# Head sums over eight offsets at once, and a first addend in another tile's memory, in a transformer block with dilated window attention and a gated MLP

## The chip, the core and the metric

The kernel runs on one core of a Trainium2 chip. A core has a matrix engine (PE, with its weight loads shown as PEld), a vector engine (DVE), a scalar engine (ACT), a general engine (POOL) and a synchronising engine (SP). They run side by side, each in the order of its own instruction list, and wait for each other by semaphores. Transfers (DMA) are issued from the lists of SP, POOL and ACT and carried by 16 shared DMA engines. The metric is the time of one execution in microseconds (us) on the device; lower is better.

## The reference

All tensors are bfloat16. There are S = 2048 positions of D = 1024 features, 32 heads of 32 features, a window of 8 offsets with a stride of 2, and a gated MLP with two halves of 1792 features.

```python
def _A_ref(x, wqkv, wo):                     # H, Dh, W, dil = 32, 32, 8, 2
    q, k, v = split_heads(x @ wqkv)
    idx = pos[:, None] - (jnp.arange(W) * dil)[None, :]
    logits = einsum('bhsd,bhswd->bhsw', q, k[idx]) * Dh ** -0.5
    attn = softmax(where(idx >= 0, logits, -1e9), axis=-1)
    return merge_heads(einsum('bhsw,bhswd->bhsd', attn, v[idx])) @ wo

def _B_ref(x, w_in, w_sp, b_sp, w_out):      # Fh = 1792
    z = gelu(x @ w_in)
    z1, z2 = z[..., :Fh], layernorm(z[..., Fh:])
    g = einsum('ts,bsf->btf', w_sp, z2) + b_sp[None, :, None]
    return (z1 * g) @ w_out

h = x + _A_ref(layernorm(x), A_wqkv, A_wo)
out = h + _B_ref(layernorm(h), B_w_in, B_w_sp, B_b_sp, B_w_out)
```

## The kernel before

**Tiling.** The positions are cut into four chunks of 512 (`NCH`, `CH`), a chunk into four row tiles of 128 (`TPC`). The projection to queries, keys and values gives feature-major tiles: a partition holds eight neighbouring features (`DLO`), so four partitions make a head. For an offset w, DVE multiplies the queries by the keys shifted by 2w (L414, `prod`) and adds the eight products of each partition together in three steps (L418, L421, L424, the last into `part`). PE then adds the four partitions of each head with a matrix of ones, `E32` (L442): that is the **head sum**, and its result is the logits `L` in PSUM. It is made of matmuls with 32 columns of weights, four of which stand side by side in the array.

**One chunk's attention.** Products and head sums (two groups of four offsets, `nw = 4`), then DVE's maximum (L451), subtraction (L461), ACT's exponential (L463), sums and reciprocal (L467 to L476), the weights `attn` (L485). PE spreads the weights of a head over its four partitions (L497, into `pb` and `pba`), ACT and DVE copy them to `AB` (L502). DVE multiplies the shifted values by them (L517) and adds (L525). Two of the eight additions are made by an accumulating transfer from POOL's queue (`gather`, L531): `av_z` is added to `av_y`, `av_zz` to `av_oT`. The tile `av_z` lies in the memory of the queries, `qT`; so the queries of the next chunk, which are loaded by POOL's queue (L387), must wait until that transfer is done (`G["qfree", c]`).

**Head.** PE multiplies the result by `wo` (`head`, L587); DVE adds the residual (L596) into `hb`, ACT sums the squares (L601), POOL makes the root (L560). Chunks 0 to 2 are normalised by ACT (L629) and go by one transpose transfer on SP's queue into `hnT` (L634). Chunk 3 is normalised row tile by row tile on DVE (L613), each with a transpose of its own (L619). The tiles `hnT` have one tag and two buffers of 8 KB a partition.

**Gated MLP.** `b_z2` (L660, four row tiles, each as a group of 1024 and one of 768 columns) makes the half that is normalised, ACT evicts it with the gelu (L667), squares it (L676) and normalises it (L689; DVE L691 for chunk 3), and it is stored. `b_z1` (L710) makes the other half, feature-major, ACT evicts it (L716), SP stores it (L717). When the head of chunk 3 is done, the attention's memory is given up, and the 12 row tiles of the normalised half of chunks 0 to 2 are loaded into it from POOL's queue (`z2sb`, L772). Then follow the mixing over positions (L810) and the output projection (L825), which have an order of their own and are the same in both kernels.

**What sets the order.** Everything between the first norm and L810 is put into a list of operations (`add`) with an engine, a length in us, dependencies and a priority. `Order.run` goes through them as a list scheduler, gives each a start by these lengths, and emits the instructions in the order of the starts. Waiting is not scheduled: an engine that is late on the chip keeps its order. So the lengths of the list set how the matmuls of head sums, heads and MLP stand among each other on PE. PE's accumulators (`acc`) are three, `L` is one, `part` two, `prod` two.

Of the kernel before, what the change touches and what calls it, by code (L numbers as in the profile page):

```python
# [11 lines left out]
BF16 = mybir.dt.bfloat16  # L12
# [8 lines left out]
P = 128  # L21
# [3 lines left out]
TPC = CH // P  # L25
KT = D // P
# [8 lines left out]
LMODE = (1, 1, 1, 1)  # L35
LSLACK, BSLACK = 2.0, 2.0
Z2ACT = (4, 4, 4, 0)
ACCUM_US = 12.0
PIECES = ((0, 0), (0, 4), (1, 0), (1, 4))
LNPRIO = (0, 2.0, 2.5, 4.0)  # L40
LAST_COLS = ((0, 512), (512, 768), (768, 1024))
# [85 lines left out]
def kernel(  # L127
# [13 lines left out]
    V, A, T = nc.vector, nc.scalar, nc.tensor  # L141
# [18 lines left out]
    E32 = csb[:, 128:160]  # L160
# [122 lines left out]
    add = o_.add  # L283
    G = {}
# [44 lines left out]
    def order():  # L329
        seq[0] += 1  # L330
        return 6.0 + seq[0] * 1e-3

    def qkv(c):
        for xi in range(3):
            wv = wsb[xi][:].rearrange("p kt (m dl) -> p kt dl m", dl=DLO)
            for dp in range(DLO // 2):
                key = ("acc", "qkv", c, xi, dp)
                deps = [G.get(("xnT", c))]
                if c == 0 and xi == 0 and dp < 2:
                    def mm(wv=wv, dp=dp):  # L340
                        if dp == 0:
                            accs = [new_acc(), new_acc()]
                            G["acc", "qkv", 0, 0, 0], G["acc", "qkv", 0, 0, 1] = accs
                            for kt in range(KT):
                                for dl in range(4):
                                    T.matmul(accs[dl // 2][:, dl % 2, :], wv[:, kt, dl, :], xnT[0][:, kt, :],  # L346
                                             start=(kt == 0), stop=(kt == KT - 1))
                    last = add("PE", 6.91 if dp == 0 else 0.0, mm, deps, prio=order(), take="acc")
                else:
                    for j, k0 in PIECES:  # L350
                        def mm(j=j, k0=k0, dl=2 * dp + j, wv=wv, key=key):
                            if j == 0 and k0 == 0:
                                G[key] = new_acc()
                            for kt in range(k0, k0 + 4):
                                T.matmul(G[key][:, j, :], wv[:, kt, dl, :], xnT[c][:, kt, :],  # L355
                                         start=(kt == 0), stop=(kt == KT - 1))
                        last = add("PE", 0.863, mm, deps, prio=order(), take="acc" if j == 0 and k0 == 0 else None)
                        deps = [(last, 0.0)]
                def ev(xi=xi, dp=dp, key=key):
                    if c == 0:  # L360
                        off = 0 if xi == 0 else HALO
                        A.copy(att_in[0][xi][:, 2 * dp:2 * dp + 2, off:off + CH], G[key][:])  # L362
                        if xi > 0 and dp == 3:
                            dma(qkv_d[xi][:, :, CH - HALO:CH], att_in[0][xi][:, :, CH:CH + HALO])
                    else:
                        stg = l1.tile([P, 2, CH], BF16, name="stg", tag="xn", bufs=4)
                        A.copy(stg[:], G[key][:])  # L367
                        dma(qkv_d[xi][:, 2 * dp:2 * dp + 2, c * CH:(c + 1) * CH], stg[:])
                G["ev", c, xi, dp] = add("ACT", 0.92, ev, [last], prio=2.0, free="acc", lat=0.15, take="xn" if c else None)
                if c:  # L370
                    dma_op(3.5, lambda: None, [G["ev", c, xi, dp]], free="xn")
            G["wdone", c, xi] = last
        G["qkvlast", c] = last
# [4 lines left out]
    def attention(c):  # L378
# [17 lines left out]
                G["xnT", 3].deps.append((d_v, 0.1))  # L396
        st, parts, qs, pvs = {}, {}, [{} for _ in range(W_WIN)], {}
        mode = LMODE[c]
        nw = 8 // max(mode, 2)
        lms = []  # L400
        first = G["avdone", c - 1] if c else None
        prev = None
        for g in range(W_WIN // nw):
            adds = []
            for wi in range(nw):
                w = g * nw + wi
                o = HALO - DIL * w
                def qk(w=w, wi=wi, o=o, g=g):
                    st = qs[w]
                    qT, kT = att_in[c][0], att_in[c][1]  # L410
                    if wi == 0:
                        parts[g] = att.tile([P, nw, mode, CH], BF16, name="part", tag="part", bufs=2)
                    st["prod"] = att.tile([P, DLO, CH], BF16, name="prod", tag="prod", bufs=2)
                    V.tensor_tensor(st["prod"][:], qT[:], kT[:, :, o:o + CH], op=ALU.mult)  # L414
                def add1(g=g, wi=wi, w=w):
                    p_ = qs[w]["prod"]
                    dst = parts[g][:, wi] if mode == 4 else p_[:, 0:4, :]
                    V.tensor_tensor(dst, p_[:, 0:4, :], p_[:, 4:8, :], op=ALU.add)  # L418
                def add2(g=g, wi=wi, w=w):
                    p_ = qs[w]["prod"]  # L420
                    V.tensor_tensor(parts[g][:, wi] if mode == 2 else p_[:, 0:2, :], p_[:, 0:2, :], p_[:, 2:4, :], op=ALU.add)  # L421
                def add3(g=g, wi=wi, w=w):
                    p_ = qs[w]["prod"]
                    V.tensor_tensor(parts[g][:, wi], p_[:, 0:1, :], p_[:, 1:2, :], op=ALU.add)  # L424
                pr_ = prev = add("DVE", 2.21, qk, [d_q, d_k, (prev, 0.0) if prev else None, first], prio=3.0, take=("prod", "part") if wi == 0 else "prod")
                pr_ = add("DVE", 1.13, add1, [pr_], prio=3.0, free="prod" if mode == 4 else None)
                if mode <= 2:
                    pr_ = add("DVE", 0.60, add2, [pr_], prio=3.0, free="prod" if mode == 2 else None)
                if mode == 1:
                    pr_ = add("DVE", 0.34, add3, [pr_], prio=3.0, free="prod")  # L430
                first = None
                adds.append(pr_)
            if g == W_WIN // nw - 1:
                G["qkdone", c] = adds[-1]
            slack = add("DMA", LSLACK if g < W_WIN // nw - 1 else 0.0, lambda: None, adds)
            def lm(g=g):
                if g == 0:
                    st["L"] = ps_att.tile([P, W_WIN, P], FP32, name="L", tag="L")
                L = st["L"]
                for z in range(mode):  # L440
                    for sq in range(4):
                        T.matmul(L[32 * sq:32 * sq + 32, nw * g:nw * g + nw, :], E32,  # L442
                                 parts[g][:, :, z, sq * P:(sq + 1) * P],
                                 start=(z == 0), stop=(z == mode - 1), tile_position=(0, 32 * sq))
            lms.append(add("PE", {1: 0.38, 2: 0.65, 4: 0.65}[mode], lm, [slack], prio=1.0, take="L" if g == 0 else None, free="part", lat=0.2))
        if c == 0:
            lms.append(add("DVE", 0.3, lambda: V.tensor_tensor(st["L"][0:32, :, 0:16], st["L"][0:32, :, 0:16], maskb, op=ALU.add),
                           lms, prio=3.0))
# [31 lines left out]
        for hw in range(2):  # L480
# [7 lines left out]
            for sh in range(2):  # L488
                def pbm(sh=sh, ws=ws, hw=hw):
# [5 lines left out]
                    for j in range(2):  # L495
                        sq = 2 * sh + j
                        T.matmul(pb[:, j], B4[32 * sq:32 * sq + 32, :], st["attn"][32 * sq:32 * sq + 32, ws, :],  # L497
                                 start=True, stop=True, tile_position=(32 * sq, 0))
                pm = add("PE", 0.2, pbm, [wait], prio=1.0, take="acc" if sh else "L", lat=0.2)
                eng = "DVE" if (hw == 0 and sh == 1) else "ACT"  # L500
                def cp(sh=sh, ws=ws, hw=hw, eng=eng):
                    (V.tensor_copy if eng == "DVE" else A.copy)(  # L502
# [2 lines left out]
                                   free="acc" if sh else "L", lat=0.15)  # L505
        last = prev
        av = {}
        homes = {"y": (att, "part", 2), "z": (att, "qT", 1), "zz": (bp, "hb", 1), "b": (att, "prod", 2), "p": (att, "prod", 2), "oT": (att, "oT", 1)}

        def mul(w, key):  # L510
            def f():
# [15 lines left out]
                    oTs[c] = av["oT"]  # L527
            return add("DVE", 2.30, f, deps, prio=3.0, free=free, lat=lat)

        def gather(to, key, deps):  # L530
            i_ = add("POOL", 1.1, lambda: nc.gpsimd.dma_start(av[to][:], av[key][:], accum_op=ALU.add, max_dma_last_dim=4096), deps, prio=1.0, lat=0.3)  # L531
            return add("DMA", ACCUM_US, lambda: None, [i_])

        y = dm(0, "y", [], take="part")
        z = dm(1, "z", [y])
        g1 = G["qfree", c] = gather("y", "z", [z])
        o_2 = dm(2, "oT", [z] + ([G["headmm", c - 1]] if c else []))
        z = dm(3, "zz", [o_2] + ([G["hnT", c - 1]] if c else []))
        g2 = gather("oT", "zz", [z])
        prev = dm(4, "b", [z], take="prod")  # L540
        for w in (5, 6, 7):
            m_ = dm(w, "p", [prev], take="prod" if w == 5 else None, free="part" if w == 7 else None)
# [22 lines left out]
    def head(c):  # L565
# [40 lines left out]
        if last:  # L606
            G["close"] = dma_op(0.0, close_, [G["headmm", c]] + [G["z2n", k, il] for k in range(c) for il in range(TPC)])
            for il in range(TPC):
# [6 lines left out]
                n_ = add("DVE", 0.5, nrm, [rs], prio=0.6)  # L615
                def tr(il=il):
                    if il == 0:
                        hnTs[c] = bp.tile([P, TPC, KT, P], BF16, name="hnT", tag="hnT")
                    nc.sync.dma_start_transpose(hnTs[c][:, il], st["hnc"][:, il, :].rearrange("s (a p) -> s a p", p=P))  # L619
                G["hnT", c, il] = dma_op(4.0, tr, [n_])  # L620
            G["hnT", c] = G["hnT", c, TPC - 1]
# [8 lines left out]
            nd.append(add("ACT", 1.16, nrm, [rs], prio=4.0))  # L630
        G["hdone", c] = nd[-1]
        def tr():
            hnTs[c] = bp.tile([P, TPC, KT, P], BF16, name="hnT", tag="hnT")
            nc.sync.dma_start_transpose(hnTs[c][:].rearrange("p il a s -> p (il a) s"),  # L634
                                        st["hnc"][:].rearrange("s il (a p) -> s (il a) p", p=P))
        G["hnT", c] = dma_op(8.0, tr, nd)
# [234 lines left out]
```

## Time and profile before

| | us |
|---|---|
| median of three runs | 732.07 |
| lowest and highest | 731.43, 734.21 |
| the profiled execution | 734.07 |
| its span | 732.2 |
| PE busy in the span | 723.2 |
| DVE busy | 419.3 |
| ACT busy | 220.8 |

The span counts from the first instruction of the program to its last; the execution's time has what lies around it too. "Busy" of PE counts overlapping matmuls once. The clock granted to PE was 0.995 of full over the span. A line of the form "L442 ... x32" is a group of 32 instructions of source line 442; "wait" is put down to the engine or transfer that ended it last. The page's lines of costliest groups give for the mixing (L810) 194.0 us of PE, for the two MLP halves (L660, L710) 98.5 and 98.4 us, and for the projections (L355) 56.6, 56.3 and 49.7 us. The head sums (L442) take 3.2 us in 32 matmuls.

### The profile page before, as it was taken

How to read it: one execution, taken by the hardware profiler on the slowest of the kernel's cores; microseconds unless marked ns; L12 is line 12 of the kernel's file. 1: busy time of each engine (PE TensorE's matmuls, PEld its weight loads, DVE VectorE, ACT ScalarE, POOL GpSimd, SP SyncE). 2: the span in 40 equal slices, each digit the busy share in tenths (PEclk: the TensorE clock that was granted, in tenths of full speed). 3: DMA queues.
4: the chain of work that ended last, by engine and by line, in shares of the span. 5: the costliest groups of instructions: out<-in, count | busy, mean ns of one | idle time of the engine just before them, and what ended most of it. 6: DMA issues, size and time to landing. Idle time of an engine off the chain costs nothing.

```text
span 732.2 us, 8410 instructions
## 1 busy us (share of the span) xinstructions
PE 723.2 (99%) x3452; PEld 367.1 (50%) x3452; DVE 419.3 (57%) x464; ACT 220.8 (30%) x269; POOL 59.0 (8%) x74
## 2 busy tenths in 40 slices
PE   7999999999999999999999999999999999999998
PEld 3666665566645344444444444444444444444444
DVE  4889999999899899989940101322232223222322
ACT  4322522544238874678654620000000000000000
POOL 0310110001201110201203000000000000000000
PEclk8999999999999999999999999999999999999999
DMA  9874398476993485383569898344105311020002
GB/s 338 311 263 112 124 235 253 145 187 204 317 372 66 150 214 166 101 233 64 123 195 295 191 283 259 111 114 131 58 30 127 117 57 42 22 90 21 1 16 71
DMA packets 115398, 113.64 MB, mean 155 GB/s; under 512 B 67904, under 2 KB 91872, under 8 KB 115232
## 3 DMA queue, kind: packets, MB, share of 16 engines
q1 hardware_dynamic: 105472, 72.63, 33.9%
q0 software_dynamic: 9456, 39.89, 18.7%
q8 instruction: 27, 0.44, 0.2%
q10 hardware_dynamic: 432, 0.59, 0.2%
q14 instruction: 11, 0.09, 0.0%
HBM read 55.09 MB, written 33.88 MB: 122 GB/s over the span
## 4 chain that ended last, share of the span: by engine, by line
PE 89%; DMA 5%; DVE 4%; issue 1%; ACT 0%; DVEq 0%
PE acc L810 26%; PE acc L355 18%; PE acc L825 13%; PE acc L710 13%; PE acc L660 10%; PE acc L587 6%; DMA qT<-qkv_d 2%; DVE prod L414 2%; DMA qkv_d<-stg 2%; PE acc L346 1%; DMA xr<-in_A_x_dram 1%; DVE prod L418 1%; DVE prod L421 0%; DMA xp<-in_A_x_dram 0%; PE tpa L255 0%
## 5 line engine op out<-in xcount | busy, mean ns | idle before, releaser
L810 PE MATMUL acc<-wspT,z2sb 128*128 128x512 bf16 x896 | 194.0, 379 | 0.0
L810 PEld LDWEIGHTS <-z2sb 128*128 128x128 bf16 x896 | 87.7, 98 | 105.7
L813 DVE TENSOR_TENSOR g<-acc,bB 128x1024 bf16<-128x1024 f32 x28 | 34.3, 1224 | 160.2 <-PE acc L810 127.6
L660 PE MATMUL acc<-win,hnT 128*128 128x512 bf16 (+1 forms) x512 | 98.5, 352 | 0.0
L710 PE MATMUL acc<-hnT,win 128*128 128x512 bf16 x448 | 98.4, 379 | 0.0
L414 DVE TENSOR_TENSOR prod<-qT,kT 128x4096 bf16<-128x4096 bf16 x32 | 72.5, 2283 | 5.2 <-ACT kT L362 2.9
L660 PEld LDWEIGHTS <-hnT 128*128 128x128 bf16 x512 | 49.8, 98 | 47.3 <-issue 0.7
L825 PEld LDWEIGHTS <-zg 128*128 128x128 bf16 x462 | 45.2, 98 | 51.8
L710 PEld LDWEIGHTS <-win 128*128 128x128 bf16 x448 | 43.4, 98 | 52.4 <-issue 1.1
L367 ACT CAST stg<-acc 128x1024 bf16<-128x1024 f32 x36 | 36.4, 1011 | 72.7 <-PE acc L355 59.2
L825 PE MATMUL acc<-wout_a,zg 128*128 128x512 bf16 (+1 forms) x264 | 58.2, 373 | 0.0
L832 DVE TENSOR_TENSOR ot<-acc,hr 128x1024 bf16<-128x1024 f32 x15 | 18.4, 1225 | 69.4 <-PE acc L825 69.4
L355 PE MATMUL acc<-xnT,wv 128*128 128x512 bf16 x256 | 56.6, 380 | 0.0
L355 PE MATMUL acc<-xnT,wk 128*128 128x512 bf16 x256 | 56.3, 379 | 0.0
L587 PE MATMUL acc<-wo_sb,av_oT 128*128 128x512 bf16 x256 | 55.9, 379 | 0.0
L355 PE MATMUL acc<-xnT,wq 128*128 128x512 bf16 x224 | 49.7, 380 | 0.0
L355 PEld LDWEIGHTS <-wk 128*128 128x128 bf16 x256 | 36.5, 144 | 18.8 <-issue 0.5
L355 PEld LDWEIGHTS <-wv 128*128 128x128 bf16 x256 | 36.5, 144 | 18.8 <-issue 0.7
L825 PE MATMUL acc<-wout_b,zg 128*128 128x512 bf16 (+1 forms) x198 | 44.4, 373 | 0.0
L587 PEld LDWEIGHTS <-av_oT 128*128 128x128 bf16 x256 | 25.1, 98 | 30.1
L355 PEld LDWEIGHTS <-wq 128*128 128x128 bf16 x224 | 31.9, 144 | 16.4 <-issue 0.7
L418 DVE TENSOR_TENSOR prod<-prod 128x2048 bf16<-128x2048 bf16 x32 | 38.3, 1216 | 0.0
(135 smaller groups left out, 565.0 us busy)
## 6 DMA issues: line engine op xcount, KB each, us to landing
qkv_d<-stg SPq DMA_DIRECT2D x36, 256.0 KB, 3.2
z_d<-z1s SPq DMA_DIRECT2D x28, 256.0 KB, 3.5
z1c<-z_d SPq DMA_DIRECT2D x28, 256.0 KB, 2.6
z_d<-u SPq DMA_DIRECT2D x12, 448.0 KB, 4.2
z2sb<-z_d POOLq DMA_DIRECT2D x12, 448.0 KB, 15.6
xr<-in_A_x_dram SPq DMA_DIRECT2D x16, 256.0 KB, 2.8
av_y<-av_z POOLq DMA_DIRECT2D x4, 1024.0 KB, 10.0
av_oT<-av_zz POOLq DMA_DIRECT2D x4, 1024.0 KB, 13.4
```

The costliest lines, as they stand in the source:

```text
L346: T.matmul(accs[dl // 2][:, dl % 2, :], wv[:, kt, dl, :], xnT[0][:, kt, :], start=(kt == 0), stop=(kt == KT - 1))
L355: T.matmul(G[key][:, j, :], wv[:, kt, dl, :], xnT[c][:, kt, :], start=(kt == 0), stop=(kt == KT - 1))
L367: A.copy(stg[:], G[key][:])
L414: V.tensor_tensor(st["prod"][:], qT[:], kT[:, :, o:o + CH], op=ALU.mult)
L418: V.tensor_tensor(dst, p_[:, 0:4, :], p_[:, 4:8, :], op=ALU.add)
L587: T.matmul(st["acc", il][:, nh, :], oTs[c][:, dl, il * P:(il + 1) * P], wo_sb[:, dl, nh * CH:(nh + 1) * CH], start=(dl == 0), stop=(dl == ...
L660: T.matmul(accf[:, n0:n1], hnTs[c][:, il, kt, :], wins[hf][:, kt, n0:n1], start=(kt == 0), stop=(kt == KT - 1))
L710: T.matmul(G["accy", c, fp][:, j, :].rearrange("p (a b) -> p a b", a=TPC), wt[:, kt, f0 * P:(f0 + 1) * P], hnTs[c][:, :, kt, :], start=(kt ...
L810: T.matmul(acc[:, j, :], z2sb[a][:, f * P:(f + 1) * P], wspT[:, a, :], start=(a == 0), stop=(a == NT - 1))
L813: V.tensor_tensor(g1[:], acc[:], bB[:, c * CH:(c + 1) * CH].unsqueeze(1).to_broadcast([P, 2, CH]), op=ALU.add)
L825: T.matmul(outs, zg[:, f, il * P:(il + 1) * P], wt[:, f0, lo:hi], start=(f == 0), stop=(f == NF - 1))
L832: V.tensor_tensor(ot[:], acc[:].rearrange("p a b -> p (a b)"), hr[:], op=ALU.add)
```

## The change

It does four things.

1. The head sums of a chunk are made once, after all eight offsets (`nw = 8`), as two rounds of four matmuls, the first over offsets 0 to 3, the second over 4 to 7. `part` holds eight offsets.
2. `av_z` of chunks 0 and 1 lies in the memory of the second `hnT` tile. For this `hnT` has two tags, `hn0` and `hn1`, of one buffer each, which the chunks take in turn.
3. The next chunk's queries wait for the accumulating transfer only after chunk 2; before, they wait for the last product (`qkdone`).
4. Lengths of the list: the first group of queries 8.4 (was 6.91), a head sum of eight 0.92 (a sum of four was 0.38), a spreading matmul pair 0.26 (was 0.2), the accumulating transfers 11.0 and 15.0 (were 12.0 each).

```diff
-ACCUM_US = 12.0
...
-                    last = add("PE", 6.91 if dp == 0 else 0.0, mm, deps, prio=order(), take="acc")
+                    last = add("PE", 8.4 if dp == 0 else 0.0, mm, deps, prio=order(), take="acc")
...
-        nw = 8 // max(mode, 2)
+        nw = 8 // mode
...
+                n = min(nw, 4)
                 for z in range(mode):
-                    for sq in range(4):
-                        T.matmul(L[32 * sq:32 * sq + 32, nw * g:nw * g + nw, :], E32,
-                                 parts[g][:, :, z, sq * P:(sq + 1) * P],
-                                 start=(z == 0), stop=(z == mode - 1), tile_position=(0, 32 * sq))
-            lms.append(add("PE", {1: 0.38, 2: 0.65, 4: 0.65}[mode], lm, [slack], prio=1.0, take="L" if g == 0 else None, free="part", lat=0.2))
+                    for w0 in range(0, nw, n):
+                        for sq in range(4):
+                            T.matmul(L[32 * sq:32 * sq + 32, nw * g + w0:nw * g + w0 + n, :], E32,
+                                     parts[g][:, w0:w0 + n, z, sq * P:(sq + 1) * P],
+                                     start=(z == 0), stop=(z == mode - 1), tile_position=(0, 32 * sq))
+            lms.append(add("PE", 0.92 if mode == 1 else 0.75, lm, [slack], prio=1.0, take="L" if g == 0 else None, free="part", lat=0.2))
...
-                pm = add("PE", 0.2, pbm, [wait], prio=1.0, take="acc" if sh else "L", lat=0.2)
+                pm = add("PE", 0.26, pbm, [wait], prio=1.0, take="acc" if sh else "L", lat=0.2)
...
-        homes = {"y": (att, "part", 2), "z": (att, "qT", 1), "zz": (bp, "hb", 1), ...}
+        homes = {"y": (att, "part", 2), "z": (bp, "hn1", 1) if c < 2 else (att, "qT", 1), "zz": (bp, "hb", 1), ...}
...
-        def gather(to, key, deps):
+        def gather(to, key, deps, us):
...
-            return add("DMA", ACCUM_US, lambda: None, [i_])
+            return add("DMA", us, lambda: None, [i_])
...
-        g1 = G["qfree", c] = gather("y", "z", [z])
+        g1 = gather("y", "z", [z], 11.0)
+        G["qfree", c] = g1 if c == 2 else G["qkdone", c]
...
-        g2 = gather("oT", "zz", [z])
+        g2 = gather("oT", "zz", [z], 15.0)
...
-            hnTs[c] = bp.tile([P, TPC, KT, P], BF16, name="hnT", tag="hnT")
+            hnTs[c] = bp.tile([P, TPC, KT, P], BF16, name="hnT", tag="hn%d" % (c % 2), bufs=1)
```

More of the change, by code (lines that the diff above doesn't have):

```diff
@@ L507, in attention @@
         av = {}
-        homes = {"y": (att, "part", 2), "z": (att, "qT", 1), "zz": (bp, "hb", 1), "b": (att, "prod", 2), "p": (att, "prod", 2), "oT": (att, "oT", 1)}
+        homes = {"y": (att, "part", 2), "z": (bp, "hn1", 1) if c < 2 else (att, "qT", 1), "zz": (bp, "hb", 1), "b": (att, "prod", 2), "p": (att, "prod", 2), "oT": (att, "oT", 1)}
         def mul(w, key):
@@ L632, in tr @@
         def tr():
-            hnTs[c] = bp.tile([P, TPC, KT, P], BF16, name="hnT", tag="hnT")
+            hnTs[c] = bp.tile([P, TPC, KT, P], BF16, name="hnT", tag="hn%d" % (c % 2), bufs=1)
             nc.sync.dma_start_transpose(hnTs[c][:].rearrange("p il a s -> p (il a) s"),
```

## The prediction

> **What bounds the kernel now.** First the busy shares, then the chain that ended last in order of time, then the waits of PE, then single lines.
>
> ```profile
> span 732.2 us, 8410 instructions
> PE 723.2 (99%) x3452; PEld 367.1 (50%) x3452; DVE 419.3 (57%) x464; ACT 220.8 (30%) x269; POOL 59.0 (8%) x74
> ```
>
> PE leaves 9 us of the span, so an edit gains only what it takes off PE's order, and loses whatever makes PE wait. The chain gives the price of a matmul and of an interruption (start, length, what):
>
> ```profile
> 63.34 0.33 PE L L442 x4
> 63.67 14.83 PE acc L355 x68
> ...
> 133.47 12.95 PE acc L355 x60
> ...
> 242.15 0.40 PE L L442 x4
> ...
> 367.93 13.81 PE acc L587 x64
> 381.75 8.63 PE acc L710 x40
> 390.38 24.33 PE acc L660 x128
> ...
> 438.88 48.35 PE acc L810 x224
> ```
>
> A full matmul costs 48.35 / 224 = 0.2158 us. The 60 of 133.47 keep that pace (12.95); the 68 behind a head sum take 14.83 against 68 x 0.2158 = 14.67, so a head sum (L442) costs 0.33 + 0.16 = 0.49 us of PE. PE's only real wait after the start is for DVE's products (total, times, longest):
>
> ```profile
> PE L L442 <- DVE part L424: 1.7, 2, 1.5
> ```
>
> From 438.88 on (the mixing over positions) nothing is edited and PE has no gap; that stretch only shifts. The other place to look is the last chunk's second norm: four transposes of `hb` into `hnT` (L619), the fourth of which goes out just after the loads of `z2sb` (L772) have begun:
>
> ```profile
> 385.50 4.40 POOL L772 DMA_DIRECT2D z2sb<-z_d  x8 [0.24 <-issue]
> ```
> ```profile
> 386.59 1.24 SPq L619 DMA_TRANSPOSE hnT<-hb  x1
> ```
> ```profile
>   PEld L660: 0.3, 1
> ...
> DMA to landing us min/median/max: 3.1/3.2/21.8
> ```
>
> The last fence is line L619: three transposes land in some 3.2 us, the slowest in 21.8, so at 386.59 + 21.8 = 408.4. L660 reaches its fourth row tile after three of them (per tile 24 full and 8 half matmuls, 28 x 0.2158 = 6.04 us): 390.38 + 18.13 = 408.5. So the transfer is hidden to within 0.1 us, and PE's weight load already waited for it once.
>
> **The change, part by part.** The order comes from the built program, the durations from the rows.
>
> *Head sums once a chunk.* Eight insertions of four matmuls become four of eight, with equal matmuls in all. A second round of four in the same insertion has no row. It costs at least one stream of 512 columns, 0.216, and at most another 0.33. So 8 x 0.49 = 3.92 becomes 4 x (0.49 + 0.216 to 0.33) = 2.82 to 3.28: a gain of 0.64 to 1.10, taken as 0.85, in the middle, as the second round changes no shape. The waits of 1.7 are both in chunk 2's two sums. The new sum stands 32 L710 matmuls behind z2 of chunk 0. I follow DVE there: chunk 2 begins some 1.2 us sooner (next part), its remaining work is the same, and five small operations on the L3 statistics (242.01 to 242.95 in DVE's rows, 0.95 us) now stand ahead of its last adds; parts are ready near 242.2, PE is there near 242.7. So the 1.7 goes; bounds: all of it back, or none. The mask, maximum and exponentials start 0.3 to 1.3 us later after each sum; behind them are the AB matmuls (L497) and DVE's values part. At chunk 3 ACT evicts one z2 accumulator and loads a table before the exponentials, so attn comes within 0.2 us of PE's L497. Cost 0 to 0.5, taken as 0 beside the middle of the first term.
>
> *First addend in the memory of the second hnT; query loads early.* av_z leaves qT for chunks 0 and 1, so the next qT load need not wait for the accumulating transfer. It removes this wait on DVE:
>
> ```profile
> 200.84 4.50 DVE L414 TENSOR_TENSOR prod<-qT,kT 128x4096 bf16<-128x4096 bf16 x2 [2.29 <-DMA qT<-qkv_d]
> ```
>
> On POOL's queue the load moves past the two accumulations and `win1`; those come no later, since the load waits for the chunk's last product (about 157 us), well before 173. PE isn't waiting for DVE at that place, so the gain is cover, worth 0 on PE. If the cover were missing, the sum's 1.7 would return. hnT's two tags alternate as its two buffers did; av_z of chunk 1 is read out long before hnT(1) is written (232 us).
>
> *Other lengths in the list* (8.4 for the first query group, 0.92 a sum, 0.26 a broadcast, 11 and 15 for the transfers). They are no instructions, but they move them. Two norms of chunk 3 go ahead of chunk 0's products, where DVE idles 2.88 us for ACT's kT copies; they need 0.9. The heads of chunks 0 to 2 move behind 4, 8 and 11 more matmuls' worth of other work, with oT ready before each by over 1 us. The one that matters is the **head of chunk 3**: 88 L710 matmuls of chunk 2 now stand ahead of it and 24 behind it, where it was 72 and 40.
>
> The head then starts at 367.93 + 16 x 0.2158 - 1.7 - 0.85 = 368.83, 0.9 later. Everything from there to the fourth transpose hangs on the head: its matmuls, DVE's residual, the norm, SP's stores and transposes in unchanged order, POOL's roots and behind them the z2sb loads. So that transpose lands 408.4 - 367.93 = 40.5 after the head's start, at 409.3. PE arrives after 13.81 + 24 x 0.2158 + 18.13 = 37.1, at 405.9. **PE now stands 3.4 us, about 405.9 to 409.3**, and what was gained is spent there: the end moves by 0.9 - 0.1 = +0.8. Bounds of this term: 16 x 0.2158 = 3.45 lost in full if the earlier terms fail, and -2.6 if the landing came 3.4 us sooner. DMA between 386 and 408 is full (busy share 1.04, 285 GB/s), so I don't expect it to.
>
> *The clock.* An idle stretch of that length meets the clock. Windows of 3.41 us aligned with the granted clock's steps (PE, PEld, DVE, ACT, POOL busy; then PEclk, DMA share, GB/s):
>
> ```profile
> 6.53:9.95 3.42, 1.48 (x18) 0.81 (x16) 3.42 (x14) 1.63 (x7) 0.00 (x0) 1.00 1.05 388
> 9.95:13.36 3.41, 2.54 (x23) 2.06 (x21) 1.35 (x4) 2.50 (x3) 0.00 (x0) 0.50 1.05 387
> 13.36:16.78 3.42, 3.42 (x10) 1.31 (x9) 0.00 (x0) 0.00 (x0) 0.00 (x0) 0.50 1.04 386
> 238.65:242.06 3.41, 1.95 (x10) 0.78 (x8) 3.38 (x7) 3.12 (x4) 0.93 (x1) 1.00 0.23 38
> ```
>
> A window with 1.48 us of matmul was followed by half clock; one with 1.95 was not. A stall of 3.4 us leaves its worse window at most 1.7, and usually under 1.48. So I expect a drop, and one full window at half rate loses 3.41 / 2 = 1.7 us. The Trainium skill ("TensorE: Matmul & The Clock Gate", "What's actually happening") says that half rate follows at least one idle window of some 3.4 us; read as a wholly empty window, a stall of this length would rarely bring it. The first row above speaks against that reading; it is a rival below.
>
> **Sum.** +0.8 + 1.7 = +2.5. The profiled execution took 734.07 (732.2 span and 1.9 around it) and would become 736.6; the median of the three runs is 732.07, 2.0 below, and I carry the difference: 734.6.
>
> **Rivals.**
> 1. *The half clock lasts two windows* (slower than before by more than a measurement can tell). The window 9.95 to 13.36 had 2.54 of 3.41 us busy and still the next was at half. So if over 0.87 us of the stall falls into the window after the drop, a second follows: up to 3.4 lost instead of 1.7, +4.2, 736.3. Place: L660's fourth tile and the first L710 behind it. For: the stall is as long as a window, so with any odd phase it lies in two. Against: when the larger part comes second, one window is enough.
> 2. *The clock stays up*: +0.8, 732.9. For: 238.65 shows that 1.95 us of work was enough. Against: that window held twice as much work as the new one will on average.
> 3. *The transpose is not late*: PE doesn't stop, 1.7 + 0.85 are kept: 729.5. For: 12 loads share 16 engines with it, and their order of service isn't shown. Against: the same transfers start at the same distances from the head.
> 4. *Products late after all*: DVE's chunk 2 isn't early, the sum of eight waits up to 1.7, which moves the head too: 2 on top of the forecast or of rival 2, 734.9 to 736.6. For: only 0.5 us of slack there. Against: 2.29 us of DVE's wait are plainly removed. (That the edits don't take effect isn't a rival: the built order has the four insertions and the early loads.)
>
> **How the numbers follow.** A difference under 0.5% (3.7 us) can't be told from no change here. Forecast 0.37, rival 1 0.32, rival 2 0.16, rival 3 0.10, rival 4 0.05. The forecast's own range is 733.7 to 735.7 (0.23 either way for the second round, up to 0.5 more at L497, up to 0.4 either way for where the stall ends in its window). Slower by over 0.5% is above 735.7: nearly all of rival 1, half of rival 4, a seventh of the forecast: 0.39. Faster is below 728.4, the low end of rival 3: 0.03. The rest, 0.58, is same. The range 731.0 to 737.4 leaves out rival 3 and the top of rivals 1 and 4.
>
> **What will show it.** L442's group: 4 insertions, waits on DVE near 0. DVE's wait on qT gone. PE's waits: one by L660 for L619 of 3 to 4 us, at 406 to 409, with the L619 maximum still about 21. The granted clock at 0.5 in the windows behind it. Wrong if the last transpose lands in under 18 us, if PE stops at another line, or if the head of chunk 3 starts before 368.

## The result, and the profile after

| | us |
|---|---|
| after, median of 15 runs | 735.43 (732.93 to 737.51) |
| before, 15 runs beside them | 732.29 (731.39 to 734.21) |
| ratio, 95% interval | 1.0038 (1.0026 to 1.0050) |
| profiled execution of after, its span | 737.51, 735.7 |

The changed kernel is 0.38% slower, some 3.1 us; 734.6 was predicted, in a range of 731.0 to 737.4. Line numbers move by -1 to +2: the head sum is now L443, the head L589, the fourth transpose L621, the two MLP halves L662 and L712, the mixing L812, the loads of `z2sb` L774.

The two longest waits of PE after the change (engine, what waited, for what: total, times, longest); the others, of 1.3 us and less, lie in the start, as the second does:

```profile
PE acc L662 <- DMA hnT<-hb: 3.2, 1, 3.2
PE tpa L254 <- DVE xn L246: 3.0, 1, 3.0
```

The waits of L442 for DVE's `part` (1.7 us) are gone. A new one stands at L662, for the fourth transpose. This transpose, with the store that its norm waits for, is all that the chain of waits has of transfers between the start and the mixing (start, length, what):

```profile
385.09 2.92 DMA h_d<-hb
388.02 0.03 issue
388.05 0.02 DVEq L615
388.07 0.05 issue
388.12 0.56 DVE hb L615
388.67 0.02 issue
388.69 21.59 DMA hnT<-hb
410.28 0.05 issue
410.32 5.96 PE acc L662 x20
```

Read upwards: PE goes on at 410.32 because the transpose landed at 410.28; it went out at 388.69 because the norm (L615) had just ended; and the norm, which writes `hb` in place, had waited for the store of that same row tile to `h_d` to land. The line of the transposes, as shown for before, now reads:

```profile
  PEld L662: 3.6, 1
  PE acc L662: 3.2, 1
...
DMA to landing us min/median/max: 3.1/3.3/21.6
```

The slowest landing has hardly changed (21.8 before). What has changed is that PE comes for it earlier. Four windows of the clock's length around it (busy us of PE, PEld, DVE, ACT, POOL; granted clock, DMA share, GB/s):

```profile
404.46:407.87 3.41, 2.67 (x17) 1.38 (x15) 0.00 (x0) 1.81 (x3) 0.54 (x1) 1.00 1.28 265
407.87:411.28 3.41, 0.96 (x5) 0.49 (x6) 0.00 (x0) 2.00 (x4) 0.00 (x0) 1.00 0.53 184
411.28:414.69 3.41, 3.41 (x10) 1.23 (x9) 0.00 (x0) 0.00 (x0) 0.00 (x0) 0.50 0.13 53
414.69:418.10 3.41, 3.36 (x21) 1.89 (x20) 0.00 (x0) 1.11 (x2) 0.00 (x0) 1.00 0.83 179
```

The window with 0.96 us of work is followed by exactly one at half clock: 3.41 / 2 = 1.7 us of work at full rate are lost there.

**What part of the 3.1 us is the change's own.** The start, which no edit touches, takes a varying time: the clock record of before has two windows at half clock in it, that of after three. These lines of PE show both ends of what follows it (start, length, engine, line), first of before, then of after:

```profile
21.73 2.54 PE L355 MATMUL acc<-xnT,wq 128*128 128x512 bf16 x11
438.72 6.64 PE L810 MATMUL acc<-wspT,z2sb 128*128 128x512 bf16 x30
```
```profile
23.14 1.03 PE L354 MATMUL acc<-xnT,wq 128*128 128x512 bf16 x4
442.25 2.97 PE L812 MATMUL acc<-wspT,z2sb 128*128 128x512 bf16 x12
```

From the first matmul of L355 (after: L354), which has the full clock in both, to the first of the mixing, before takes 438.72 - 21.73 = 417.0 us and after 442.25 - 23.14 = 419.1. That is +2.1 for the change itself. This measure, the *stretch* below, leaves the start's chance out, and everything that was edited lies in it.

The runs say nearly the same. Each run's mean granted clock tells how many windows it spent at half, and no run of after had fewer than one; in its profile one of them is the new one. Runs of after with one, two and three such windows took 733.8, 734.7 and 736.2 (medians of 3, 4 and 7); 31 runs of before beside a later experiment took 732.0, 732.9 and 734.5 with none, one and two (8, 13 and 9). At equal starts that is +1.7 to +1.8.

### The profile page after: what moved, and what is told of

It is laid out like the page before. It is cut to its first block, busy times and chain, and to the rows that moved or that the text cites. A ratio compares the mean times of both kernels' runs of the same rounds, so it can differ in the third digit from the quotient of the medians.

```text
span 735.7 us, 8354 instructions
## 1 busy us (share of the span) xinstructions
PE 720.6 (98%) x3392; PEld 368.1 (50%) x3452; DVE 420.1 (57%) x464; ACT 221.4 (30%) x269; POOL 60.9 (8%) x74
## 3 DMA queue, kind: packets, MB, share of 16 engines
q0 software_dynamic: 9456, 39.89, 18.9%
## 4 chain that ended last, share of the span: by engine, by line
PE 94%; DMA 4%; issue 1%; DVE 1%; DVEq 0%
PE acc L812 26%; PE acc L354 22%; PE acc L827 13%; PE acc L712 12%; PE acc L662 11%; PE acc L589 7%; DMA hnT<-hb 3%; PE acc L345 1%; DMA xp<-in_A_x_dram 1%; PE tpa L254 0%; DMA h_d<-hb 0%; PE pb L498 0%; PE L L443 0%; DVE bnst L226 0%; DVE bnst L227 0%
## 5 line engine op out<-in xcount | busy, mean ns | idle before, releaser
L812 PE MATMUL acc<-wspT,z2sb 128*128 128x512 bf16 x878 | 193.1, 379 | 0.9
L812 PEld LDWEIGHTS <-z2sb 128*128 128x128 bf16 x896 | 87.7, 98 | 105.7
L662 PE MATMUL acc<-win,hnT 128*128 128x512 bf16 (+1 forms) x501 | 99.6, 356 | 3.8 <-DMA hnT<-hb 3.2
L712 PE MATMUL acc<-hnT,win 128*128 128x512 bf16 x448 | 98.0, 379 | 0.0
L662 PEld LDWEIGHTS <-hnT 128*128 128x128 bf16 x512 | 50.2, 99 | 52.4 <-DMA hnT<-hb 3.6
L712 PEld LDWEIGHTS <-win 128*128 128x128 bf16 x448 | 43.6, 98 | 52.5 <-issue 0.8
L366 ACT CAST stg<-acc 128x1024 bf16<-128x1024 f32 x36 | 36.5, 1013 | 70.0 <-PE acc L354 64.4
L354 PE MATMUL acc<-xnT,wk 128*128 128x512 bf16 x253 | 56.1, 379 | 0.3 <-issue 0.2
L354 PE MATMUL acc<-xnT,wv 128*128 128x512 bf16 x251 | 55.9, 379 | 0.4 <-issue 0.2
L589 PE MATMUL acc<-wo_sb,av_oT 128*128 128x512 bf16 x250 | 55.6, 379 | 0.3
L354 PE MATMUL acc<-xnT,wq 128*128 128x512 bf16 x217 | 49.1, 380 | 0.4
L354 PEld LDWEIGHTS <-wk 128*128 128x128 bf16 x256 | 36.6, 144 | 18.9 <-issue 0.7
L354 PEld LDWEIGHTS <-wv 128*128 128x128 bf16 x256 | 36.6, 144 | 18.7 <-issue 0.5
L354 PEld LDWEIGHTS <-wq 128*128 128x128 bf16 x224 | 32.0, 144 | 16.6 <-issue 0.7
L589 PEld LDWEIGHTS <-av_oT 128*128 128x128 bf16 x256 | 25.0, 98 | 30.1
L669 ACT ACTIVATE u<-acc 128x1024 bf16<-128x1024 f32 (+1 forms) x32 | 29.3, 916 | 33.3 <-PE acc L662 33.1
```

The source lines that it names most:

```text
L589: T.matmul(st["acc", il][:, nh, :], oTs[c][:, dl, il * P:(il + 1) * P], wo_sb[:, dl, nh * CH:(nh + 1) * CH], start=(dl == 0), stop=(dl == ...
L662: T.matmul(accf[:, n0:n1], hnTs[c][:, il, kt, :], wins[hf][:, kt, n0:n1], start=(kt == 0), stop=(kt == KT - 1))
L669: A.activation(st["u", il][:, hf * 1024:hf * 1024 + wd], G["accz", c, il, hf][:].rearrange("p a b -> p (a b)")[:, 0:wd], ACTF.Gelu_apprx_t ...
L712: T.matmul(G["accy", c, fp][:, j, :].rearrange("p (a b) -> p a b", a=TPC), wt[:, kt, f0 * P:(f0 + 1) * P], hnTs[c][:, :, kt, :], start=(kt ...
L812: T.matmul(acc[:, j, :], z2sb[a][:, f * P:(f + 1) * P], wspT[:, a, :], start=(a == 0), stop=(a == NT - 1))
```

## The experiments

The theory: the two edits do what they are meant to do; the loss is PE's wait for the fourth transpose and the half clock behind it. It has three links: the head of chunk 3 has too little work behind it, the transpose is slow beside the loads of `z2sb`, and the idle window slows the clock.

**The loads behind the transpose.**

`G["tr3"]` is the fourth transpose.

```diff
             zl.append(dma_w(z2sb[i][:], z2_d[i * P:(i + 1) * P, :]))
+        tc.add_manual_dep(zl[0].ins, G["tr3"].ins.name, wait_for, ...)
```

> The changed kernel, but the first load of z2sb waits until the fourth transpose of the last chunk's hb has landed; nothing else moves. Theory: the changed kernel loses 3.2 us to PE's wait for that transpose, which is slow only beside the loads, and 1.7 us to the half clock behind the wait. Both go: 735.4 - 3.2 - 1.7 = 730.5, the transpose lands in about 3.3 us, the clock stays at 1.0 after 405. Rival A, the transpose is slow by itself or for another transfer: 735.4 with the wait still there. Rival B, the loss of the changed kernel lies elsewhere (head sums, memory): the wait goes but the time stays over 734. Rival C, the loads come 4 us later and the mixing then waits for wspT: PE gains at 406 and waits at the first L812.

Measured: 729.83, ratio to before 0.9959 (0.9944 to 0.9974). The waits of PE that are left and the line of the transposes:

```profile
PE tpa L254 <- DVE xn L246: 2.4, 1, 2.4
PE wps L209 <- DVE warm L206: 1.3, 1, 1.3
PE acc L345 <- DVE xnT L255: 0.9, 1, 0.9
PE acc L354 <- issue: 0.4, 2, 0.2
```
```profile
DMA to landing us min/median/max: 3.0/3.1/3.6
```

All four waits lie in the start. The transpose that took 21.6 us takes 3.6 at most, and the clock stays up. The stretch is 414.4: 4.7 us less than after, where 3.2 + 1.7 = 4.9 was expected, and 2.6 less than before. So what the edits gain was there all the time. `wspT` landed at 418.9 and the mixing began at 434.9: the later loads cost nothing.

**The same on the kernel before.**

> The kernel before with the same one wait added (first load of z2sb behind the fourth transpose). Theory: there the transpose was hidden to within 0.1 us, so the time stays at 732.3, within 0.3. Rival, the loads cost PE something in other ways as well (stores, evictions, the shared transfers): 1 us or more is gained here too.

Measured: 733.36, ratio 1.0008 (0.9993 to 1.0023); stretch 417.4. The transpose landed 21.9 us after the head's start for 40.7, and it brought nothing: in the kernel before it was hidden.

**Work in place of the wait.**

```diff
+                        if c == NCH - 1 and il == 3 and hf == 0 and part == 0:
+                            for r in range(16):
+                                T.matmul(accf[:, 0:CH], hnTs[c][:, 2, r % KT, :], wins[0][:, r % KT, 0:CH], start=True, stop=True)
```

> The changed kernel with 16 more matmuls of PE (row tile 2 against the first window again, overwritten by the true start of row tile 3) just ahead of row tile 3 of the last chunk's z2: 16 x 0.2158 = 3.45 us of work where PE waited 3.25. Theory: the wait is filled, the clock never falls, so in spite of 3.45 us more work the time is 735.4 + 0.2 - 1.7 = 733.9. Rival A, the half clock costs nothing or comes anyway: 735.6. Rival B, the wait isn't at this place or moves along: 738.9.

Measured: 733.48, 1.0005 (0.9992 to 1.0018): 16 matmuls more than after, and 2 us faster. The same three windows:

```profile
404.46:407.87 3.41, 3.41 (x20) 1.78 (x19) 0.00 (x0) 1.89 (x4) 0.00 (x0) 1.00 0.95 162
407.87:411.28 3.41, 3.36 (x17) 1.56 (x16) 0.00 (x0) 0.83 (x2) 0.00 (x0) 1.00 0.29 108
411.28:414.69 3.41, 3.41 (x21) 1.81 (x19) 0.00 (x0) 1.11 (x2) 0.00 (x0) 1.00 1.17 262
```

The transpose still lands late (21.5 us), but PE is busy and the clock stays at 1.00. The stretch is 417.6, 1.5 under after's: the half clock's share, by itself.

**Part of the wait filled** (`range(4)` in the lines above).

> The changed kernel with 4 more matmuls (0.86 us) ahead of row tile 3, for 16 in the run before: a wait of 2.4 us is left. Its worst window is idle for 1.2 to 2.4 us, by phase. Windows with 1.48 of 3.41 us busy (1.9 idle) were followed by half clock, with 1.95 (1.5 idle) not. Theory: the half clock comes in about 7 runs of 10, and the time is 735.4 in these and 733.7 in the others. Rival A, only a window without any work brings it: 733.7 in all. Rival B, any wait over 2 us brings it: 735.4 in all.

Measured: 734.64, 1.0024 (1.0009 to 1.0039). This kernel also has `range(4)` for `range(16)` where the constants are made, and so leaves out the mask behind the first four positions; apart from the 4 matmuls its instructions are those of after. In its profile 2.0 us of wait are left and the clock stays up; the window that holds most of the wait:

```profile
405.66:409.08 3.42, 1.90 (x9) 0.90 (x10) 0.00 (x0) 1.42 (x2) 0.00 (x0) 1.00 0.41 152
```

With 1.90 us of work there was no drop. How many of the other eleven runs had one can't be told from their mean clocks, as the start's windows are in them too; so the shares of 7 and 3 in 10 stay untested.

**The head's place.** `deps = [(G["avdone", c], -1.7) if last else G["avdone", c]]` puts the head eight matmuls earlier, 3.6 for -1.7 sixteen later.

> The changed kernel with the head of chunk 3 eight matmuls earlier (80 L712 ahead of it and 32 behind, for 88 and 24). Its input was ready 1.57 us before the head began, and 8 matmuls are 1.73, so PE waits at most 0.2 there. Theory: the fourth transpose still lands 40.5 us after the head's start, PE comes 38.8 after it: a wait of 1.6 us for 3.25, and with at least 1.8 us of work in each window the clock stays up: 735.4 - 1.6 - 1.7 = 732.1; with the clock down 733.8. Rival, the place of the head doesn't matter: 735.4.

Measured: 731.85, 0.9987 (0.9967 to 1.0007), stretch 415.7. The wait shrinks, the clock stays up:

```profile
  PEld L662: 1.5, 1
  PE acc L662: 1.1, 1
...
DMA to landing us min/median/max: 3.0/3.3/21.2
```

So the first link holds. Eight matmuls moved behind the head took 3.4 us off the stretch: the wait is 2.1 us shorter, and the half clock is gone.

> The changed kernel with the head of chunk 3 sixteen matmuls later (104 L712 ahead, 8 behind). Theory: the transpose still lands 40.5 us after the head's start, so the wait grows by 16 x 0.2158 = 3.45 to 6.7 us, longer than the clock's window. With one window at half clock 735.4 + 3.45 = 738.9; with two, 740.6. Rival, the place of the head doesn't matter or the landing is tied to the loads' clock time and not to the head: 735.4 to 736.

Measured: 734.17, 1.0010 (0.9996 to 1.0025), faster than after: **the expectation failed**, by 4.7 us. PE waited only 2.7 us:

```profile
  PEld L662: 3.1, 1
  PE acc L662: 2.7, 1
...
DMA to landing us min/median/max: 3.1/3.1/18.4
```

The transpose landed 36.5 us after the head's start and not 40.5. The clock stayed up. The landing is not tied to the head; what sets it was open here.

**Each edit alone.**

> The kernel before with the memory edit alone (av_z of chunks 0 and 1 in hnT's second buffer, query loads waiting for the last product and not for the accumulation); PE's order is the one of before, head of chunk 3 at 72 and 40. Theory: PE's waits of 1.7 us for DVE's part in chunk 2 go, since DVE loses its wait of 2.3 for qT, and everything behind moves 1.7 us up, head and transpose with it: 732.3 - 1.7 = 730.6. Rival A, DVE is given back the time before chunk 2 and the wait stays: 732.3. Rival B, the earlier loads disturb other transfers: over 733.

Measured: 730.55, 0.9973 (0.9959 to 0.9986), stretch 415.1 against 417.0: the waits of 1.7 went, as expected. The order is that of before, 40 L710 behind the head, and the transpose is hidden.

> The kernel before with the head sums of eight offsets alone, without the memory edit; its order also has 88 L710 matmuls ahead of the last head and 24 behind, so the first load of z2sb waits for the fourth transpose here too, to keep that wait out. Theory: the sums save PE 8 x 0.47 - 4 x 0.70 = 1.0 us, but DVE is 2.3 us later in chunk 2 than in the changed kernel, and one insertion must wait for all eight offsets: a wait of about 2 us for part. 729.8 + 2 = 731.8. Rival, the single sum is late enough in the order to need no early loads: no wait, 729.8.

Measured: 729.89, 0.9957 (0.9942 to 0.9973), no wait for `part`: the rival was right. In chunk 2 the single sum stands behind 32 L712 matmuls, where the second of two stood behind 16, so PE comes to it 16 x 0.2158 = 3.5 us later in its order. DVE is there just in time without the early loads; its wait for `qT` was 0.6 us here and not 2.3. How close it is shows in the next kernel, sums_alone, which has the same order (its lines for PE, then DVE):

```profile
235.86 7.07 PE L712 MATMUL acc<-hnT,win 128*128 128x512 bf16 x32
242.86 0.71 PE L444 MATMUL L<-part,csb 128*32 128x512 bf16 x8
```
```profile
242.69 0.43 DVE L424 TENSOR_TENSOR part<-prod 128x512 bf16<-128x512 bf16 x1
```

The sum begins 0.26 us before its last part is done (242.69 + 0.43 = 243.12): only its second round needs that part.

> The kernel before with the head sums of eight offsets alone: neither the memory edit nor the load held back. The order has 88 L710 matmuls ahead of the last head and 24 behind. Theory: the planned length of the single sum alone moves the head, so the wait for the fourth transpose and the half clock appear without the memory edit: 729.9 (the same with the load held back) + 3.2 + 1.7 = 734.8. Rival, the early query loads of the memory edit are what makes the transpose late: 730.

Measured: 730.03, 0.9969 (0.9957 to 0.9980): no wait again, and no half clock behind the start. **The expectation of 734.8 failed**, though PE's order at the end is the changed kernel's, 88 and 24. The line of its transposes:

```profile
DMA to landing us min/median/max: 3.1/3.1/16.6
```

It went out 18.2 us after the head's start for 18.9, and landed at 34.8, before PE came at 37.1.

**Why 16.6 in one and 21.6 in the other.** The DMA records between the third row tile's norm and the fourth transpose, first of after (385 to 388.2), then of sums_alone (383.8 to 387):

```profile
q14 instruction: 1, 0.01, 1.2%
...
h_d<-hb SPq DMA_DIRECT2D x1, 256.0 KB, 2.9
```
```profile
q1 hardware_dynamic: 1212, 0.54, 70.8%
...
h_d<-hb SPq DMA_DIRECT2D x1, 256.0 KB, 2.3
```

In after one 8 KB packet of instructions is fetched there, and the store of `h_d` takes 2.9 us; in sums_alone the window has no such packet, and it takes 2.3. In the profiles of all fourteen kernels it goes this way: where an instruction packet lies 16.3 to 17.1 us after the head's start (eleven, before and after among them) the store lands at 18.1 to 18.3; where it lies elsewhere (three) at 17.5 to 17.6. The norm waits for that store, the transpose for the norm. The loads on POOL's queue don't wait for it, so the transpose goes out 1.1 us behind the first load instead of 0.5. The last experiment takes the store out of the way (`from_` is chosen as `to` is):

```diff
+                    to = st["xr", il][:] if il == TPC - 1 else st["hnc"][:, il, :]
-                    V.tensor_scalar(st["hnc"][:, il, :], st["hnc"][:, il, :], ...)
+                    V.tensor_scalar(to, st["hnc"][:, il, :], ...)
...
-                    nc.sync.dma_start_transpose(hnTs[c][:, il], st["hnc"][:, il, :].rearrange(...))
+                    nc.sync.dma_start_transpose(hnTs[c][:, il], from_.rearrange(...))
```

> The changed kernel, but the norm of the last chunk's fourth row tile writes into the memory of its xr and not over hb, so neither it nor the transpose waits for the store of h any longer; nothing else moves. In the profiles the fourth transpose takes 19 to 21 us to land where it goes out 18.8 to 18.9 us after the head's start and 1.1 us behind the first load (before, after, four experiments), and 15 to 16 us where it goes out at 18.1 to 18.3 and 0.4 to 0.5 us behind it (head_16_later, sums_alone). In the first group the store of h that the norm waits for lands at 18.2, with an 8192-byte instruction packet in the DMA records at 16.3 to 17.1; in the second at 17.5, without one. Theory: being 0.7 us earlier against the loads is worth 4 to 5 us of landing. Then the transpose goes out near 18.1 and lands at 34.5 to 36.5 after the head's start, before PE's 37.1: no wait, no half clock, 730.5. Rival, the two groups differ by something else (the address of hnT, the packet itself): the transpose goes out 0.7 us earlier and lands 0.7 earlier, a wait of 2.5 us, 733 to 734.7.

Measured: 731.16, 0.9973 (0.9962 to 0.9984). The norm, and the line of the fourth transpose:

```profile
384.70 0.55 DVE L616 TENSOR_SCALAR xr<-hb,l_3nmean,l_3rstd 128x1024 bf16<-128x1024 bf16 x1 [0.66 <-POOL l_3rstd L562]
```
```profile
DMA to landing us min/median/max: 3.0/3.3/17.4
```

It waits 0.66 us for the root, where in after it waited 1.44 us for the store. The transpose goes out at 18.1 and lands at 35.4, though the instruction packet still lies at 16.3. So 0.8 us of earlier issue bring the landing 5.0 us forward, and PE doesn't wait. That the packet delays the store is seen only side by side; the step from the store to the wait is shown by the edit.

**Loads in smaller pieces.** The DMA records of after while the fourth transpose was under way (389.9 to 410.3):

```profile
q0 software_dynamic: 901, 5.16, 84.9%
q1 hardware_dynamic: 1250, 0.45, 15.8%
```

The loads (queue 0) hold the engines for 84.9% of the time, the transpose and a store (queue 1) for 15.8%. The transpose's packets are small and many. If they pass one by one between the large ones, smaller load packets let them through sooner. To test that, each load is split in two, or in four:

```diff
-            zl.append(dma_w(z2sb[i][:], z2_d[i * P:(i + 1) * P, :]))
+            for n in (0, 896):
+                zl.append(dma_w(z2sb[i][:, n:n + 896], z2_d[i * P:(i + 1) * P, n:n + 896]))
```

> The changed kernel with each z2sb load as two loads of 896 columns, nothing held back. In the records of the changed kernel the fourth transpose is 1024 packets of 256 bytes, 64 for each DMA engine, and between its issue and its landing 720 load packets of 7168 bytes and 0.383 us ran: about one load packet (0.28 us or more) between two of its own. Theory: the engines alternate packet by packet, so packets of half the size halve the wait: 64 x (0.19 + 0.02) = 13 us instead of 20.4, landing near 403, no wait of PE, no half clock: 730.5. Rival A, the engines share by bytes or serve in order of issue: landing still near 410, 735.4. Rival B, twice as many load issues hold POOL or the loads up, and the mixing starts late: over 732 with a new wait behind 435.

Measured: 729.57, 0.9960 (0.9947 to 0.9973), no wait of PE, stretch 414.1:

```profile
DMA to landing us min/median/max: 3.0/3.3/7.5
```

Cutting the loads ends the wait: 7.5 us, where some 14 were expected. But it isn't shown to be the size of the packets. The 12 whole loads are 768 packets of 7168 bytes; cut in two they are 768 of 5376 and 384 of 3584, two thirds of the size in the mean and not half. And the transpose doesn't alternate with them: its 1024 packets start between 2.7 and 4.9 us after its issue, with 73 load packets among them, where in after they start between 3.9 and 20.4 us, with 565 among them. So 14 of the transpose's packets pass for each load packet, and it is through in some 2 us. POOL issues a half load every 0.58 us and a whole one every 0.55, so with halves it asks for some half of the bytes in the same time; whether this is the reason wasn't separated.

> The same with four loads of 448 columns each. Theory, alternation packet by packet: 64 x (0.10 + 0.02) = 7.5 us, or less if POOL's 0.54 us for each of 48 issues thins the loads out: landing near 397; the time stays at 730.5, since PE had nothing more to win after the halves. Rival A as above: landing near 410, 735.4. Rival B: the loads end over 48 x 0.54 = 26 us after their start and wspT behind them, at the latest near 426; the mixing starts at 437, so no wait is expected from it.

Measured: 737.78, 1.0056 (1.0029 to 1.0082), **slower, against the expectation**. The transpose landed in 6.0 us, and the profiled execution is among the fastest of its runs, 731.17, with no wait of PE between the start and the mixing; nearly all of its other runs took over 734. The clock isn't it: at a mean clock of 0.995 its runs took up to 738.2, and the one of loads_in_halves 731.5. What they lose isn't in that profile, and it stays open.

All of them side by side. "Behind" is L712 matmuls behind the last head; out and landed are those of the fourth transpose, in us from the head's start; the wait is PE's for it; all but the ratio are of the profiled execution.

| kernel | ratio to before | behind | out, landed | wait | stretch |
|---|---|---|---|---|---|
| before | 1 | 40 | 18.8, 40.7 | 0 | 417.0 |
| after | 1.0038 | 24 | 18.9, 40.5 | 3.2 | 419.1 |
| loads_behind_after | 0.9959 | 24 | 18.9, 21.9 | 0 | 414.4 |
| loads_behind_before | 1.0008 | 40 | 18.8, 21.9 | 0 | 417.4 |
| fill_the_wait | 1.0005 | 24 | 18.9, 40.4 | 0 | 417.6 |
| fill_4 | 1.0024 | 24 | 18.8, 40.1 | 2.0 | 417.1 |
| head_8_earlier | 0.9987 | 32 | 18.9, 40.1 | 1.1 | 415.7 |
| head_16_later | 1.0010 | 8 | 18.1, 36.5 | 2.7 | 417.4 |
| memory_alone | 0.9973 | 40 | 18.8, 39.4 | 0 | 415.1 |
| sums_alone_loads_behind | 0.9957 | 24 | 18.3, 21.3 | 0 | 414.1 |
| sums_alone | 0.9969 | 24 | 18.2, 34.8 | 0 | 414.2 |
| last_norm_apart | 0.9973 | 24 | 18.1, 35.4 | 0 | 414.9 |
| loads_in_halves | 0.9960 | 24 | 18.9, 26.4 | 0 | 414.1 |
| loads_in_quarters | 1.0056 | 24 | 18.8, 24.8 | 0 | 414.1 |

Three versions beat both kernels by about the same, within their intervals: the changed kernel with its loads behind the transpose or in halves, and the head sums alone with the loads behind.

## Why the prediction was right, point by point

- **Head sums and waits, a gain of 1.7 + 0.85.** From the starts of PE's matmuls, an insertion of four holds its stream up by 0.43 us and one of eight by 0.64 (0.91 in chunk 0). The eight of before come to 5.28 us with their waits, the four of after to 2.84: a gain of 2.44 for 2.55. But the reason given for the 1.7 was too narrow. I took it from the early query loads; either edit alone removes the waits (memory_alone, sums_alone), the sums by standing later in PE's order. And the 0.5 us between DVE and PE weren't there: in after the sum begins at 244.16 us and its last part is done at 244.20. That this is no wait rests on the second round alone needing that part, which I hadn't counted on; here the prediction was lucky.
- **The memory edit, worth 0 on PE.** Alone it is worth 1.9 on the stretch, as the cover that it gives removes the waits. Beside the merged sums it adds nothing: 414.4 with both, 414.1 with the sums alone, loads held back in both. What it gains, the sums have gained already.
- **Head of chunk 3 0.9 later:** 346.7 us after the start of the stretch, for 346.0, so 0.65. I put the move down to the other lengths in the list; the sums with their length of 0.92 alone give the same 88 and 24 (sums_alone).
- **The fourth transpose, a wait of 3.4 us at 405.9 to 409.3.** It came to 3.2, one wait, at that line, some 1 us later as the start was. It was the step that decided: the landing of 40.5 after the head's start was met to 0.1 us. Part of that is luck. I took the landing as fixed to the head, and it is no constant: 34.8 to 36.5 where the transpose goes out 0.7 us sooner. Before and after have the instruction packet at nearly the same place (17.1 and 16.3 us after the head's start), which I hadn't looked at; that this packet makes the 0.7 us is seen only side by side. Had the transpose gone out 0.7 us sooner, rival 3 (729.5) would have been the result, as sums_alone (730.0) shows with the same order of PE at the end. The chance of 0.10 for it was given for the wrong reason and was probably too low.
- **One window at half clock, 1.7 us.** Exactly one came, and filling the wait gave 1.5 to 1.7 back. Rival 1, a second window, didn't come in the profile: most of the wait fell into one window, and the one behind it was full. Rival 2 rested on the Trainium skill ("TensorE: Matmul & The Clock Gate", "What's actually happening"), read as a wholly idle window of some 3.4 us. The trace doesn't agree with that reading: 0.96 us of work were in the window, and half clock followed. The bound that I took from before (half clock behind 1.48 us of work, none behind 1.95) was met with room, but it isn't sharp, as the last section shows.
- **The sum, +2.5.** The stretch grew by 2.1, runs with equal starts by 1.7 to 1.8, the medians by 3.1. The rest of the 3.1 is the start, which drew longer in those 15 runs.

## What to carry to other kernels

An edit that saves time ahead of a hidden transfer brings the consumer forward, and only where the transfer's own chain comes forward too is the saving kept; look up how close each hidden transfer is to its consumer (here 0.1 us) before counting a gain. Two edits that each gain 2 to 3 us may remove the same wait, and what they move besides can still add up to a loss. Where a small transfer has to pass a bulk load, let the load wait for it or cut the load once: here either was worth some 5 us of after's stretch for 0 us of PE, while cutting it in four made most runs slower.

## What the runs showed of the hardware

- A transpose of one row tile landed in 3.0 to 3.6 us without POOL's loads and in 16.6 to 21.8 beside whole ones. The Trainium skill ("DMA: Bandwidth & Descriptors", "Queues, rings and completion order") says that each engine takes the queues in turn, a packet at a time. The records don't follow this one for one: among the transpose's 1024 packets start 565 load packets in after, and 73 with halves. Whether a packet of the records is one in the page's sense, no run here shows.
- Being 0.6 to 0.8 us sooner at issue went with a landing 4 to 5.7 us sooner (head_16_later, sums_alone, last_norm_apart). In the packet records of these three, 371 to 526 of the transpose's packets start in the first 6 us, and 268 in after; but 450 do in head_8_earlier, which lands late. So why is open.
- An 8 KB packet of instructions beside a 256 KB store goes with 0.65 us more for that store (2.9 for 2.3), and where in the program it falls moves with a few instructions.
- The clock fell behind windows of 3.41 us with 0.96 us of work (after) and 1.48 (before, at the start), and stayed up behind 1.63 (head_16_later), 1.90 (fill_4) and 2.31 (head_8_earlier). But no bound on PE's work in one window fits all profiles. At the start, it fell behind 1.63 us in sums_alone and stayed up behind 1.42 in last_norm_apart. Two windows of each, with the granted clock third from the end (those of last_norm_apart are counted back from the half clock behind its last instruction):

```profile
7.00:10.41 3.41, 1.63 (x22) 1.19 (x22) 3.37 (x15) 1.65 (x5) 0.00 (x0) 1.00 1.05 386
10.41:13.83 3.42, 2.54 (x18) 1.57 (x15) 1.01 (x2) 2.10 (x3) 0.00 (x0) 0.50 1.05 388
```
```profile
4.73:8.15 3.42, 1.42 (x7) 0.45 (x5) 3.42 (x12) 2.48 (x5) 0.00 (x0) 1.00 1.05 395
8.15:11.56 3.41, 2.27 (x32) 1.80 (x32) 2.75 (x10) 2.45 (x5) 0.00 (x0) 1.00 1.05 386
```

What else counts is open.
